# A fused attention and low-rank mixer kernel: eight seven-product pairs in each of batches 1 to 3, low-rank steps shared by two head pairs, part of one VectorE add moved to ScalarE, and a new written-out order

## The chip, the cores and the metric

The kernel runs on one core of one Trainium2 chip. The core has a matrix engine (TensorE, PE in the profile; its weight loads stand in a row of their own, PEld), VectorE (DVE), ScalarE (ACT), GpSimd (POOL) and a queue engine (SyncE, SP). Each runs its own instructions in the order in which they were issued and waits for others through semaphores. TensorE writes to PSUM, eight banks of 512 fp32 values on each of 128 partitions. The metric is the device time of one execution in microseconds (us). It was taken three times without the profiler, and once more with it.

## What is computed

Attention with a band of 96 positions and 8 global keys, for 4 batches, 8 heads, 768 positions and 64 values per head, and behind it a mixer: a low-rank product over positions (768 to 32 to 768) that is added to the attention's output, and a two-layer perceptron (512 to 2048 to 512) with a skip connection.

```python
# attention
scores = scale * np.matmul(q, k.transpose(0, 1, 3, 2)) + bias
scores = np.where(keep, scores, -1000000000.0)
a = np.exp(scores - max); a = a / (sum(a) + 1e-09)
attn = np.matmul(a, v)                    # 4 x 8 x 768 x 64
# mixer, x = attn as 4 x 768 x 512
xt = x.transpose(0, 2, 1)
h = xt @ U @ V                            # U 768 x 32, V 32 x 768
u = x + h.transpose(0, 2, 1)
out = u + np.maximum(u @ w_ch1, 0.0) @ w_ch2
```

## The kernel before

**Units of work.** Work is cut into tasks, each for one engine: a Python function that issues one to 22 instructions. A planner (`Planner.run`) goes through the task names in the order of the list `ORDER`, gives each the earliest start that its engine, its inputs and its buffers allow by costs written beside it (duration, `lat`, `lead`), and picks a buffer or PSUM bank for it. The tasks are then issued by planned start. So on each engine the tasks run in the order of `ORDER`; the costs set only the choice of banks and buffers and the order between engines in the program's text. The chip's own waits decide when each really starts.

**Attention.** Two heads form a pair; there are four pairs in a batch, numbered 0 to 15 through the four batches. For pair p: `lk`, `lq`, `lv` load keys, queries and values (GpSimd queue, with a cast to fp16); `TK`, `TQ` transpose on TensorE for pairs 0 to 7, and `EK`, `EQ` take the result out of PSUM; for pairs 8 to 15 `EK` and `EQ` are DMA transposes on SP's queue. `KO`, `VC`, `VG` make shifted copies of keys and values. `SB` and `S` are the scores, `EX` the exponential (ScalarE), `MK` a mask (VectorE), `PV` the product with the values, `RC` and `NM` the normalization into `x_sb`, `XC` a cast to fp16.

**Low-rank part.** `UP` multiplies a pair's cast output by U (six matmuls of 32 columns); `XE` copies the 32 columns four times side by side (ScalarE or VectorE), `XU` turns them on TensorE, `TE` copies them into `tmp`, and `HM` multiplies with V in row tiles of 32 partitions. From pair 4 on, `XT` turns the cast output itself with a DMA transpose (SP's queue) into `uT`, and `E0`, `E1` (line 1053 for a batch's last pair, line 1065 for the others) add the low-rank term from PSUM onto it with VectorE. `HM` is done for two pairs at once from pair 4 on.

**Perceptron.** The first layer multiplies `uT` by `w1` in 16 blocks of 128 hidden units, over two halves of 384 positions. Batch 0 does it plainly (`M1`, then `RL`, `RM` on ScalarE). In batches 1 to 3, blocks are taken in pairs (z and z+8) as 2 x 2 block products with seven products instead of eight (`ZP1` to `ZP7`, two matmuls of 384 columns each, line 1197), which need sums of weights (`ZS`) and of `uT` (`ZT`) from VectorE, three copies out of PSUM by ScalarE (`ZU`, `ZW`, `ZX`, line 410), three VectorE results (`ZA`, `ZB`, `ZD`, line 1214) and one ScalarE result (`ZR`, line 1242). Batch 1 has six such pairs and four plain blocks (hidden blocks 0, 1, 8 and 9), batches 2 and 3 have eight pairs. The second layer is done the same way in all batches: `Sa` to `Sd` are sums of hidden values (VectorE, line 1259), `RS` puts the low-rank term into PSUM first (line 1302), `P1` to `P7` are the products, each of eight matmuls of 256 columns (line 1319), for three blocks of positions t, and `DA` to `DH` (lines 1331, 1350, 1363) add them onto `x_sb`. `O` stores 128 positions (SP's queue).

**Names.** `P43.2b` is product 4 of batch 3, block 2, second half; `ZP21.4` is product 2 of batch 1, pair 4. Four tilings of TensorE occur: full (most), 64 rows (`S`), 32 rows (`HM`, `RS`) and one for the transposes of pairs 1 to 3.

## Time and profile before

| | |
|---|---|
| three executions without profiler | 214.19, 214.19 and 213.17 us (median 214.19) |
| the profiled execution | 213.56 us |
| its span, first to last instruction | 211.8 us |
| TensorE busy | 204.8 us (97%), 2231 matmuls |
| VectorE busy | 185.6 us (88%), 382 instructions |
| ScalarE busy | 135.2 us (64%), 255 instructions |
| GpSimd busy | 74.2 us (35%) |
| granted TensorE clock | 0.998 |

The page lists busy time by engine, the span in 40 slices, the DMA queues, the chain of work that ended last, and groups of instructions by source line with their mean duration. The duration of a matmul in the profile holds its way through the array, so neighbours overlap: what a run of matmuls costs is the length of the run in the chain, divided by their number. Further views give the busy time of each engine in chosen windows, the chain in order of time, waits with their releasers, and the time from a DMA's issue to its landing.

### The profile page before, as it was taken

What the parts mean: (1) busy time and instruction counts of PE and PEld (TensorE: products, weight loads), DVE (VectorE), ACT (ScalarE), POOL (GpSimd) and SP (SyncE); (2) the same over time, 40 slices, a digit from 0 to 9 for tenths busy, and PEclk for the clock granted to TensorE, in tenths of its full rate; (3) what the DMA queues carried; (4) which work ended last, traced back from release to release, by engine and by line L of the source; (5) the groups of instructions that cost most, each with busy time, mean ns of one, the idle gap of its engine ahead of it and who ended that gap; (6) DMA issues with size and microseconds to landing.
All of it is one profiled execution on the core that took longest, in us unless ns stands there. A gap on an engine that the chain in (4) does not pass through costs nothing.

```text
span 211.8 us, 5602 instructions
## 1 busy us (share of the span) xinstructions
PE 204.8 (97%) x2231; PEld 146.0 (69%) x2231; DVE 185.6 (88%) x382; ACT 135.2 (64%) x255; POOL 74.2 (35%) x98
## 2 busy tenths in 40 slices
...
GB/s 182 161 173 167 181 166 168 187 200 206 158 161 129 154 172 195 247 108 161 79 127 165 113 170 151 165 60 52 64 30 47 40 0 184 19 0 0 64 186 151
DMA packets 102330, 27.22 MB, mean 129 GB/s; under 512 B 90272, under 2 KB 99424, under 8 KB 102304
## 3 DMA queue, kind: packets, MB, share of 16 engines
...
q1 hardware_dynamic: 30112, 13.28, 30.1%
q8 instruction: 17, 0.28, 0.6%
...
HBM read 27.75 MB, written 6.29 MB: 161 GB/s over the span
## 4 chain that ended last, share of the span: by engine, by line
PE 83%; DMA 9%; POOL 3%; DVE 2%; issue 1%; POOLq 0%; DVEq 0%
PE ps L1319 33%; PE ps L1197 24%; PE ps L1103 9%; PE ps L774 4%; PE ps L1127 4%; DMA uT<-x 3%; DMA vt<-in_v_dram 3%; DMA stgk<-in_k_dram 2%; PE ps L908 2%; PE ps L907 2%; PE ps L1302 2%; PE ps L645 1%; PE ps L891 1%; PE ps L1020 1%; POOL stgq L501 1%
## 5 line engine op out<-in xcount | busy, mean ns | idle before, releaser
L839 ACT ACTIVATE ep<-ps 128x1024 f16<-128x1024 f32 (+1 forms) x48 | 44.3, 956 | 16.6 <-PE ps L774 16.4
L1319 PEld LDWEIGHTS <-htr 128*128 128x128 f16 x392 | 36.6, 98 | 6.4 <-issue 1.6
L1331 DVE TENSOR_TENSOR x_sb<-x_sb,ps 128x256 f32<-128x256 f32 (+1 forms) x60 | 26.5, 463 | 3.9 <-PE ps L1319 3.5
L410 ACT ACTIVATE zu<-ps 128x384 f32<-128x384 f32 x50 | 23.4, 497 | 9.8 <-PE ps L1197 6.4
L1319 PEld LDWEIGHTS <-sA 128*128 128x128 f16 x288 | 26.7, 97 | 3.7 <-issue 0.6
L1214 DVE CUSTOM_DVE_ANT_0 htr<-ps,zu 128x384 f16<-128x384 f32 x50 | 26.3, 550 | 1.8 <-PE ps L1197 1.8
L505 POOL DMA_DIRECT2D stgq<-in_q_dram x24 | 20.0, 852 | 21.6 <-DMA qT<-stgq 18.3
L1319 PE MATMUL ps<-w,sA 128*128 128x256 f16 x192 | 24.6, 273 | 0.0
L1197 PEld LDWEIGHTS <-w 128*128 128x128 f16 x176 | 16.8, 98 | 10.8 <-issue 0.2
L505 POOL DMA_DIRECT2D stgk<-in_k_dram x24 | 20.2, 857 | 11.5 <-DMA kT<-stgk 8.5
L1319 PE MATMUL ps<-w,htr 128*128 128x256 f16 x192 | 24.0, 273 | 0.0
L1319 PE MATMUL ps<-tB,htr 128*128 128x256 f16 (+1 forms) x200 | 23.3, 268 | 0.0
L1103 PE MATMUL ps<-uT,w 128*128 128x384 f16 x112 | 20.5, 326 | 0.0
L1197 PE MATMUL ps<-uT,w 128*128 128x384 f16 x88 | 19.5, 326 | 0.0
L1197 PE MATMUL ps<-zt,w 128*128 128x384 f16 x88 | 19.2, 326 | 0.0
L509 POOL DMA_DIRECT2D vt<-in_v_dram x16 | 16.8, 1058 | 4.0 <-PE ps L774 2.0
L852 DVE TENSOR_TENSOR ep<-ep,mask 128x1024 f16<-128x1024 f16 x24 | 16.3, 682 | 0.9 <-ACT ep L839 0.9
L946 DVE TENSOR_TENSOR x_sb<-ps,rcp 128x768 f32<-128x768 f32 x16 | 15.2, 953 | 0.4
L1103 PEld LDWEIGHTS <-w 128*128 128x128 f16 x112 | 10.5, 98 | 6.7
L1197 PE MATMUL ps<-zt,zs 128*128 128x384 f16 x64 | 14.6, 326 | 0.0
L774 PE MATMUL ps<-qT,kT 64*128 64x128 f16 x192 | 14.3, 218 | 0.0
L1109 ACT ACTIVATE htr<-ps 128x384 f16<-128x384 f32 x28 | 13.0, 495 | 1.9 <-PE ps L1103 1.5
...
## 6 DMA issues: line engine op xcount, KB each, us to landing
out_dram<-x_sb SPq DMA_DIRECT2D x22, 256.0 KB, 2.4
...
stgk<-in_k_dram POOLq DMA_DIRECT2D x24, 96.0 KB, 5.7
stgq<-in_q_dram POOLq DMA_DIRECT2D x24, 96.0 KB, 5.7
w<-in_moe_w_ch_dram POOLq DMA_DIRECT2D x8, 256.0 KB, 6.3
w<-in_moe_w_ch_dram POOLq DMA_DIRECT2D x4, 512.0 KB, 11.5
...
```

Of the source, the lines that this page charges most:

```text
L410: nc.scalar.activation(dst, src, AF.Copy)
L505: nc.gpsimd.dma_start(o[:, i], src[b, h0 + i].rearrange("(n p) d -> p n d", p=P))
L509: nc.gpsimd.dma_start(vt[gv.slot][:, :, :, 0:D], v[b, h0:h0 + 2].rearrange("h (n p) d -> p h n d", p=P),)
L774: nc.tensor.matmul(t[:, hi, j * P:(j + 1) * P], lhs, qt[r, i * P:(i + 1) * P], start=not biased, stop=True, skip_group_check=biased,)
L839: nc.scalar.activation(ep[gep.slot][:, :, lo:512], ps[:, gsc.slot:gsc.slot + 2, lo:512], AF.Exp, scale=qk_scale)
L852: nc.vector.tensor_tensor(ev, ev, mv, ALU.mult)
L946: nc.vector.tensor_tensor(xo, pvo()[:, :, :, 0:D], rcp[p % 2].unsqueeze(3).broadcast_to((P, 2, NB, D)), ALU.mult)
L1103: nc.tensor.matmul(ps[:, g.slot, 0:HS], w1[:, dc, jt * P:(jt + 1) * P], ub[:, dc, i * HS:(i + 1) * HS], start=(dc == 0), stop=(dc == NDC - 1),
L1197: nc.tensor.matmul(bank(g), a()[:, i], bq[:, i], start=first and i == 0, stop=last and i == 1, skip_group_check=True,)
L1214: return lambda: nc.vector._custom_dve(TENSOR_ADD_SAT, out=o, in0=x(), in1=y(), s0=3.0e38, s1=0.0)
L1319: nc.tensor.matmul(o if part is None else o[:, part], a[:, j, c0 + cols.start:c0 + cols.stop], bq[:, j] if part is None else bq[:, j, part ...
L1331: nc.vector.tensor_tensor(o, o, x, ALU.add)
```

## The change

- **Seven-product pairs.** Batch 1 takes all eight pairs with seven products; its four plain blocks and their `RL`, `RM` go. The sums `ZS0` of the weights, made in batch 2 before, are made in batch 1.
- **Shared low-rank steps.** Two neighbouring pairs put their `UP` results side by side (64 columns) into one PSUM bank of their own; one `XE`, `XU` and `TE` serve both (sixteen of each become eight), and `HM` is done for two pairs everywhere (ten become eight). `tmp` and `td` shrink to half. `DF` says which pair of the two comes first.
- **`RS`** changes from four matmuls of 32 rows and 256 columns to eight of 64 rows and 128 columns, with zeros in the rows of V that do not belong (`vz` and a longer `vs2` on VectorE make them once).
- **Low-rank term.** For nine pairs (`EA`) ScalarE copies the term from PSUM into an fp16 buffer (`AH`), and VectorE adds it from there (`E0`).
- **Engines of single tasks.** On VectorE no longer: `EK1 EK5 EK7 EQ1 EQ3 EQ7 KO7` and `VC10 VG10 VC15 VG15` (to ScalarE), `VC9 VG9 KO9` (to SP's queue); newly on VectorE: `EK3 EK6 KO11 KO14 VC6 VG6 XC10 XC15` (from ScalarE), `VC12 VG12` (from SP). `VC14 VG14` go from ScalarE to SP, `KO15` from SP to ScalarE.
- **Planner.** Other constants, a cost for early matmuls, another rule for SP's DMAs, one more filling matmul in gaps at the start.
- **Order.** `ORDER` is new throughout. Below are the places that the text speaks of.

The diff, cut to these parts:

```diff
 ORDER = """
...
-UP5 P30.0 DF0.1 MK7.0 EQ8 DF0.0 XT4 UP4 P50.2 XE4 P60.1 EK10 DA0.2 Sc0.1 XU4 ZS2 P60.2 PV7 XE5 TE4 RC7 DB0.2 NM7 XC6
-UP6 XE6 P60.0 XU5 XU6 TE5 P50.0 P70.2 DB0.1 lk11 DC0.0 TE6 DD0.2 XC7 P70.1 DB0.0 HM5 UP7 XE7 P40.2 P70.0 XU7 VC11 KO10
-TE7 KO8 XT6 XT7 E04 DD0.1 lk12 P50.1 DG0.2 E05 DD0.0 HM7 DC0.2 P40.0 P40.1 E06 S8.1 E17 E07 DG0.1 DG0.0 O0.0 lq9 DC0.1
-EK9 lv8 lq10 EX8.2 EX8.1 M1a1.1 O0.2 ZT1 M1b1.1 S8.0 M1b1.5 ZS3 EX8.0 ZP11.5 ZP11.6 lv9 ZP11.7 RM1.5 lv10 ZP21.5 ZU1.5
...
-P63.2 DC3.1 O2.3 O2.4 DF3.0 P33.1 DB3.2 DB3.1 O2.5 DF3.1 DD3.0 O2.0 P73.2 P73.1 DD3.2 O3.2a O2.1 O3.0 P43.0 DD3.1 O3.1
-O2.2 P43.1 P43.2a DG3.0 O3.5a DG3.1 DG3.2a O3.3 O3.4 P33.2 O3.5b DH3.2 O3.2 P43.2b DG3.2b O3.5c
...
+SB3.0 S3.2 S3.0 VC2 VG2 EX2.0 RC0 NM0 PV2 VC3 VG3 XC0 EX3.2 RC2 NM2 XC2 EX3.0 SB3.1 S3.1 UP0 EX3.1 UP1 w1_1 lq5 PV3.0
+PV3.1 lq4 XE1 lk4 XU1 TE1 w1_2 TQ5 w1_3 HM1 lv6 w1_0 lv5 lk5 PV3.2 TQ4 lv4 w1_5 lk6 w1_6 w2_2 w1_4 EQ5 E00 w1_7 E01
+w2_0 lq6 RC3.1 RC3.0 NH3.0 NH3.1 RC3.2 NH3.2 UP2 UP3.0 UP3.1 UP3.2 EQ4 XE3 mask1 NM3 TK4 XU3 M1a0.2 TE3 vz HM3 EK4 E02
+M1c0.2 M1a0.3 E13 M1c0.3 M1d0.3 E03 M1b0.3 M1d0.2 mask3 KO4 M1b0.7 mask2 M1b0.2 RL0.3 RL0.2 S4.1 EX4.1 M1b0.5 RM0.5
+M1b0.4 EX4.2 M1a0.1 M1a0.6 M1b0.6 TK5 RM0.7 M1a0.7 RM0.4 RL0.6 MK4.1 vs2 MK4.2 VC6 VC4 VG6 VG4 ZS1 VC5 RL0.7 mask4 EK5
...
+PV6 VC7 DF0.0 EX7.1 XC5 TWb1 P50.0 P30.2 XC4 RC6 NM6 S7.0 RS0.1 EX7.0 XT5 EQ8 MK7.2 EK8 MK7.1 VG7 DA0.2 MK7.0 P20.1
+DF0.2 XT4 P10.1 DC0.2 PV7 UP5 XC6 UP4 RC7 P30.1 UP6 XE5 DA0.1 XU5 P60.1 NM7 XC7 DF0.1 Sc0.1 DB0.1 P60.2 TE5 HM5 AH4
+UP7 AH5 XT7 P60.0 P50.1 ZS3 XT6 lk11 XE7 DB0.2 XU7 TE7 P70.1 E04 HM7 DB0.0 KO8 AH6 lv9 P70.2 lq11 E05 lv12 lq10 lq9
+ZP11.5 E17 E07 S8.1 EX8.1 ZU1.5 DD0.1 P70.0 P40.1 ZP11.0 ZP11.4 VC8 DD0.2 E06 EX8.2 ZP21.4 ZT1 DC0.0 ZP21.5 ZA1.5 VC9
+EK11 ZP61.5 DG0.1 DD0.0 VC10 ZW1.5 P40.2 DC0.1 ZP21.0 ZU1.4 ZP71.5 ZU1.0 P40.0 ZA1.4 ZA1.0 ZX1.5 ZP61.4 ZW1.4 DG0.0
+ZP51.5 DG0.2 ZB1.5 O0.2 S8.0 EX8.0 ZP11.6 ZP71.4 ZP41.5 O0.1 ZP31.5 ZP21.2 TD1 EK10 ZS0 ZP11.2 VG10 EK9 O0.0 ZX1.4
...
+P73.1 P33.0 DD3.1 DF3.0 DG3.2a O3.1 P43.1 P33.2 O3.0 DH3.2 P73.0 O3.5a O3.5b DG3.1 DD3.0 P43.2b DG3.2b O3.2 O3.4 O3.5c
+P43.0 DG3.0 O3.3
...
-    "Z": ((1, (2, 3, 4, 5, 6, 7)), (2, (0, 1, 2, 3, 4, 5, 6, 7)), (3, (0, 1, 2, 3, 4, 5, 6, 7))),
-    "ZK": (2, 3, 0, 1),
+    "Z": ((1, (0, 1, 2, 3, 4, 5, 6, 7)), (2, (0, 1, 2, 3, 4, 5, 6, 7)), (3, (0, 1, 2, 3, 4, 5, 6, 7))),
+    "ZK": [2, 3, 0, 1],
...
-    "TE": "AAADADAAAADAAADA",
-    "XE": "ADDAAAAAAAAAAAAA",
-    "EK": "ADDADDADAADAAAAD",
-    "EQ": "DDADADADADADAAAA",
-    "KO": "ADDDDDDDADAAASAS",
+    "TE": "AAAAAAAAAADAAADA",
+    "XE": "AADAAAADAAAAAAAA",
+    "EK": "AADDDADAAADAAAAD",
+    "EQ": "DAAAADAAADADAAAA",
+    "KO": "ADDDDDDAASADASDA",
...
-    "VO": "DDDDDDAADDDASAAD",
-    "XC": "DDDDAAAAAAAAQAAA",
+    "VO": "DDDDDDDADSAADASA",
+    "XC": "DDDDAAAAAADAQAAD",
...
-    "H2": [4, 6, 8, 10, 12, 14],
-    "R2": {0: (), 1: (), 2: (), 3: ()},
     "SG": [2, 2, 2, 4],
+    "EA": [4, 5, 6, 8, 9, 10, 12, 13, 14],
+    "DF": [0, 0, 1, 0, 0, 0, 0, 0],
...
-    OVER = {ACT: 0.105, DVE: 0.08}
+    COLD = 4.9
+    OVER = {ACT: 0.12, DVE: 0.09}
...
+            if t.eng == PE and s < self.COLD:
+                t.dur = min(2 * t.dur, t.dur + self.COLD - s)
...
-                    behind = max(0.0, dma_free[POOL] - s - 0.8)
-                    begin = max(s + t.lead, dma_free[SP])
-                    dma_free[POOL] = max(dma_free[POOL], begin) + need
-                    dma_free[SP] = begin + need
-                    t.end = begin + need + min(0.7 * behind, 6.0) + (1.1 if late else 0.3)
+                    behind = max(0.0, dma_free[POOL] - s)
+                    dma_free[POOL] = max(dma_free[POOL], s + t.lead - 0.8) + need
+                    t.end = s + t.lead + min(0.8 * behind, 6.5) + (0.4 if late else 0.1)
                     clock[SP] += min(0.08 * behind, 0.6)
...
-    tmp = sb("tmp", [P, DM], FP16, 2)
+    tmp = sb("tmp", [P, 2 * P], FP16, 2)
...
-    td = sb("td", [P, hd], FP16)
+    td = sb("td", [P, P], FP16)
...
+    c_vz = add(DVE, 0.55, lambda: nc.vector.memset(vs[:, 1:3], 0.0), name="vz")
...
-            o = vs[VR[g]:VR[g] + 2 * R, g]
-            if g < 2:
-                for i in range(2):
-                    nc.gpsimd.dma_start(o[i * R:(i + 1) * R], moe_V[:, g * HS:(g + 1) * HS])
-            else:
-                nc.vector.tensor_tensor(o, vf[:, 0:HS], vf[:, HS:S], ALU.subtract)
+            for i in range(2):
+                if g < 2:
+                    r = slice(64 * g + i * R, 64 * g + (i + 1) * R)
+                    nc.gpsimd.dma_start(vs[r, 0], moe_V[:, g * HS:(g + 1) * HS])
+                else:
+                    r, r2 = slice(i * R, (i + 1) * R), slice(64 + i * R, 64 + (i + 1) * R)
+                    nc.vector.tensor_tensor(vs[r, 1 + i], vf[r, 0:HS], vf[r, HS:S], ALU.subtract)
+                    nc.vector.tensor_copy(vs[r2, 1 + i], vs[r2, 0])
         return go
...
-        gu = Group("ps", 1, among=MLP1) if turned else gx
+        k = p % 2
+        if k == 0:
+            shared[p // 2] = Group("ps", 1, among=MLP1), Group("xu")
+        gu, gxu = shared[p // 2]
+        leads = CFG["DF"][p // 2] == k
 
         def low(a, b):
-            if turned:
-                return ps[:, gu.slot, a:b]
-            return ps[:, gx.slot + a // P, 384 + a % P:384 + a % P + b - a]
+            return ps[:, gu.slot, a:b]
 
...
-                        low(0, R), xx[:, c], u16[:, c],
-                        start=turned and c == 0, stop=(c == NB - 1), skip_group_check=True,
+                        low(k * R, (k + 1) * R), xx[:, c], u16[:, c],
+                        start=leads and c == 0, stop=(c == NB - 1), skip_group_check=True,
...
-        def hmix(k=0, gx=gx):
+        def hmix(gx=gx):
             for half in (0, 1):
                 r = slice(64 * half + R * k, 64 * half + R * (k + 1))
                 nc.tensor.matmul(
-                    ps[:, gx.slot + half, 0:HS], tmp[b % 2][r, hp * P:(hp + 1) * P], vs[r, half],
+                    ps[:, gx.slot + half, 0:HS], tmp[b % 2][r, hp // 2 * P:(hp // 2 + 1) * P], vs[r, 0],
                     start=turned, stop=True, skip_group_check=True,
...
+            f_, l_ = (ups[p], ups[p - 1]) if leads else (ups[p - 1], ups[p])
+            l_[0].deps.append(f_[-1])
+
+            def xuevac():
+                copy(
+                    ENG[CFG["XE"][p]], xus[gxu.slot].rearrange("p (g x) r -> p g (x r)", g=2),
+                    low(0, 2 * R).unsqueeze(1).broadcast_to((P, 2, 2 * R)),
+                )
+
+            def xuturn():
+                nc.tensor.matmul(
+                    low(P, 2 * P), xus[gxu.slot].rearrange("p g r -> p (g r)"), ident16, start=True, stop=True, skip_group_check=True,
+                )
+
+            def tevac():
+                copy(ENG[CFG["TE"][p]], tmp[b % 2][:, hp // 2 * P:(hp // 2 + 1) * P], low(P, 2 * P))
+
+            XE = add(ENG[CFG["XE"][p]], 0.28, xuevac, [f_[-1], l_[-1]], acq=[gxu], name=f"XE{p}")
+            XU = add(PE, 0.06, xuturn, [XE], lat=0.22, rel=[gxu], name=f"XU{p}")
+            TE = add(ENG[CFG["TE"][p]], 0.29 if CFG["TE"][p] == "D" else 0.3, tevac, [XU] + xw, rel=[gu], name=f"TE{p}")
+            other, og = waiting[p - 1]
+
+            def hboth():
+                other()
+                hmix()
+
+            HM = add(
+                PE, 0.19, hboth, [TE, c_vs[0], c_vs[1]], lat=0.22, acq=[og, gx] if turned else [], mode=2, name=f"HM{p}",
+            )
+            tmp_done[p - 1] = tmp_done[p] = TE
 
         def evacs(HM, gx=gx, turned=turned, XT=XT):
             w = mm1_done[b - 2] if b >= 2 else []
...
+            elif p in CFG["EA"]:
+                gh = Group("zu")
+
+                def low_copy():
+                    nc.scalar.activation(
+                        zu[gh.slot].bitcast(FP16).rearrange("p (h c) -> p h c", h=2), ps[:, gx.slot:gx.slot + 2, 0:HS], AF.Copy
+                    )
+
+                def low_add():
+                    o = uT[b % 2][:, hp]
+                    nc.vector.tensor_tensor(o, o, zu[gh.slot].bitcast(FP16), ALU.add)
+
+                AH = add(ACT, 0.81, low_copy, [HM], acq=[gh], rel=[gx], name=f"AH{p}")
+                ut_done[p] = (add(DVE, 0.555, low_add, [AH] + w + XT, rel=[gh], fast=2, name=f"E0{p}"),)
...
-            def rest(k, t, gXY=gXY):
-                gX, gY = gXY[t]
-                cols = slice(t * P, (t + 1) * P)
+            def rest(gX=gX, gY=gY, cols=cols):
                 for i in range(2):
-                    for n, g, m in ((1, gX, td if i else tb[:, 0:hd]), (2, gY, tb[:, i * hd:(i + 1) * hd])):
-                        r = slice(VR[n] + k * R, VR[n] + (k + 1) * R)
-                        yield half(g, i), vs[r, n, cols], m[r], i == 0
-
-            duo = CFG["R2"].get(b, ())
-
-            def rests(ts):
-                def go():
-                    for steps in zip(*(rest((k + ts[0]) % 2, t) for k, t in enumerate(ts))):
-                        for o, l, r, first_ in steps:
-                            nc.tensor.matmul(o, l, r, start=first_, stop=False, skip_group_check=True)
-                return go
-
-            if t not in duo[1:]:
-                ts = duo if t in duo else (t,)
-                RS = add(
-                    PE, 0.23 * (1.1 if t in duo else 1), rests(ts), [TD] + mm1_done[b][-1:] + c_vs, lat=0.3,
-                    acq=[g for u in ts for g in gXY[u]], mode=2, name=f"RS{b}.{t}",
-                )
-                rs_done[b].append(RS)
-                rs_of.update({(b, u): RS for u in ts})
-            RS = rs_of[b, t]
+                    for k in range(2):
+                        for r, g, m in ((slice(64, P), gX, td if i else tb[:, 0:P]), (slice(0, 64), gY, tb[:, i * P:(i + 1) * P])):
+                            nc.tensor.matmul(
+                                half(g, i)[:, k * P:(k + 1) * P], vs[r, 1 + k, cols], m[r], start=i == 0 and k == 0, stop=False, skip_group_check=True,
+                            )
+
+            RS = add(PE, 0.23, rest, [TD] + c_vs, lat=0.22, acq=[gX, gY], mode=1, name=f"RS{b}.{t}")
+            rs_done[b].append(RS)
 
...
-                    idle(int(gap / 0.43), 512, bank)
+                    idle(int(gap / 0.43 + 0.6), 512, bank)
...
```

198 lines of the change are left out of this document (84 added, 114 removed).

## Prediction

> **What bounds the kernel now.** I read the page's busy times first, then its summary of the chain, then the busy time of each engine in windows.
>
> ```profile
> PE 204.8 (97%) x2231; PEld 146.0 (69%) x2231; DVE 185.6 (88%) x382; ACT 135.2 (64%) x255; POOL 74.2 (35%) x98
> ...
> PE 83%; DMA 9%; POOL 3%; DVE 2%; issue 1%; POOLq 0%; DVEq 0%
> ```
> ```profile
> 15.00:20.00 5.00, 4.56 (x91) 2.81 (x88) 4.43 (x11) 4.51 (x7) 5.00 (x7) 1.00 2.26 171
> ...
> 70.00:80.00 10.00, 8.94 (x97) 6.89 (x96) 8.54 (x18) 5.41 (x10) 7.68 (x9) 1.00 2.15 161
> 80.00:90.00 10.00, 10.00 (x67) 5.89 (x66) 9.86 (x25) 8.00 (x18) 1.64 (x2) 1.00 1.68 225
> 90.00:100.00 10.00, 10.00 (x130) 6.20 (x129) 9.65 (x21) 9.80 (x18) 4.29 (x5) 1.00 1.53 133
> 100.00:110.00 10.00, 10.00 (x129) 7.86 (x127) 9.93 (x16) 7.64 (x15) 8.12 (x10) 1.00 1.50 109
> ```
>
> The columns are the window, its length, then busy time and instructions of PE, PEld, DVE, ACT and POOL, then the granted clock. TensorE is the bound: it stands in 83% of the chain, and from 80 us on it has no hole. It has holes in the start, where GpSimd issues loads without pause, and in one place between 70 and 80 us. But VectorE is nearly as full as TensorE in batch 1 (9.65 to 9.93 of 10). So a saving on TensorE counts in full only while VectorE keeps up. The chain in order of time (start, length, what) gives the hole and the prices:
>
> ```profile
> 27.27 0.65 PE ps L1127 x4
> ...
> 54.81 0.32 PE ps L1302 x4
> 55.13 0.98 PE ps L1319 x8
> ...
> 66.67 0.06 PE ps L1000
> ...
> 71.32 6.52 DMA uT<-x
> 77.93 1.03 DVE uT L1053 x2
> 79.00 1.46 PE ps L1127 x8
> ...
> 123.09 0.55 PE ps L774 x16
> ...
> 166.28 0.87 PE ps L1319 x8
> 167.16 0.27 PE ps L1020 x4
> 167.43 0.98 PE ps L1319 x8
> ...
> 172.01 17.23 PE ps L1197 x106
> 189.23 0.71 PE ps L1302 x12
> ...
> 208.45 0.29 DVE x_sb L1350
> ```
>
> **TensorE's own work.** A matmul of 384 columns costs 17.23 / 106 = 0.163 us. Eight blocks of a product cost 0.87 when the array keeps its tiling and 0.98 behind an `HM` or `RS`: leaving another tiling costs 0.11. Entering costs about the same: three `RS` together take 0.71, alone each 0.32, so 0.25 goes with two interruptions. I take 0.10 for each change of tiling.
> - Two more seven-product pairs: 32 matmuls of the first layer become 28, 4 x 0.163 = -0.65.
> - `XU`: eight fewer, six of them behind the start, 6 x 0.06 = -0.35.
> - Changes of tiling, counted by walking the two lists with the tilings of `S`, `RS`, `HM` and the early transposes: 101 before and 81 after in all; from the first task of layer one 70 and 60. `RS` now has the tiling of `S` and often stands next to it. 10 x 0.10 = -1.0.
> - `RS` itself: two matmuls run at once in different rows in both forms. Sixteen `S` matmuls of 128 columns take 0.55 with one change of tiling, 0.056 a couple, so eight take 0.22; four of 256 columns take 0.32 - 0.10 = 0.22. No difference.
>
> Against the last point stands a rule of the Trainium skill ("TensorEngine Tiling (Array Packing)", Instruction Overhead): each matmul carries some 60 cycles of overhead, so one should not cut a dimension that is small already. Read as an addition of 25 ns each (60 cycles at the 2.4 GHz that the Trainium skill gives in "Trainium Kernel Development and Optimization", NeuronCore Architecture), two more couples in each of twelve blocks would add an estimated 0.6 us, and the forecast would be 0.6 later. The trace speaks against that reading: a couple of 128 columns takes 0.056 us, half of what one of 256 columns takes.
>
> Together -2.0 us behind the start.
>
> **The hole at 78 us.** The last cast of batch 0 (`XC7`) ends at 71.3, its DMA transpose lands 6.52 us later, VectorE adds (`E17`, `E07`, 1.03), and TensorE starts layer one at 79.00 after 1.1 us of idleness.
>
> ```profile
> PE ps L1127 <- DVE uT L1053: 1.1, 1, 1.1
> ```
> ```profile
> DMA to landing us min/median/max: 2.7/4.3/7.1
> ```
> ```profile
> 67.80 5.33 SPq L987 DMA_TRANSPOSE uT<-x  x2
> ```
>
> In the new order I add up what TensorE has between the end of `XC7` and the first task that needs the transposes. By the list `XC7` ends some 3.4 us after `PV7` starts. `P40.1` stands 10.0 us of TensorE work after `PV7`, so the cover is 6.6 us. `P40.1` needs `DD0.1`, which VectorE has queued behind `E17` and `E07`: landing + 0.55 + 0.55 + 0.41, less overlaps, about landing + 1.3. At a landing of 6.5 us the stall is 1.3, as before; at the median of 4.3 there is none. `XT6` is now issued behind `XT7` on SP and blocks `E06` and with it `ZP21.4`, which has 1.5 us more cover. Fewer loads are queued just ahead of `XT7` than before, so I take a landing of 5.7 and a stall of 0.5: -0.7 (ends -1.24 and +0.3).
>
> At the other two batch boundaries there is no hole now. `XT11` stands behind `EK12` on SP and `DD1.1` behind `E111`, `E011`; `XT15` stands behind `XT13`, and `DD2.0` behind `E115`. With landings as above this gives nothing to 1.5 us in sum; +0.4.
>
> **VectorE and ScalarE.** The nine low-rank adds, the extra products and the moves of tasks are priced by these rows (mean ns after the comma):
>
> ```profile
> L1065 DVE TENSOR_TENSOR uT<-uT,ps 128x768 f16<-128x768 f16 x9 | 8.4, 949 | 0.4 <-issue 0.2 <-PE ps L1020 0.2
> L1156 DVE TENSOR_TENSOR zt<-uT,zt 128x768 f16<-128x768 f16 x3 | 1.7, 557 | 0.1
> L1214 DVE CUSTOM_DVE_ANT_0 htr<-ps,zu 128x384 f16<-128x384 f32 x50 | 26.3, 550 | 1.8 <-PE ps L1197 1.8
> L412 DVE COPY vo<-vt 32x660 f16<-32x660 f16 x10 | 4.6, 463 | 0.1
> L412 DVE COPY vo<-vt 128x660 f16<-128x660 f16 x10 | 4.0, 407 | 0.8 <-DMA vt<-in_v_dram 0.8
> L412 DVE COPY qT<-ps 128x768 f16<-128x768 f16 x4 | 3.0, 746 | 3.9 <-PE ps L645 3.9
> L412 DVE CAST x<-x_sb 128x768 f16<-128x768 f32 x3 | 1.6, 542 | 0.0
> L1179 DVE TENSOR_TENSOR w<-w 128x512 f16<-128x512 f16 x4 | 1.7, 425 | 0.1
> ```
> ```profile
> L410 ACT ACTIVATE uT<-ps 128x768 f16<-128x768 f32 x3 | 2.4, 811 | 0.1
> L410 ACT ACTIVATE xus<-ps 128x128 f16<-128x128 f32 x14 | 3.8, 276 | 7.9 <-PE ps L891 7.8
> ```
>
> An add that reads PSUM takes 0.949, one of the same shape from SBUF 0.557: nine pairs give VectorE -3.5. Six more `ZA`, `ZB`, `ZD` cost 6 x 0.55 = +3.3. Of `EK` and `EQ` four more leave than come, -3.0; five `XE` and `TE` go, -1.4; two `XC` come, +1.1; `vz` and the longer `vs2` are about three more copies like those of 0.4, +1.3; one `VC`, `VG` couple goes, -0.9. In all about -3.1, mostly in the start and in batch 0. ScalarE gets 9 x 0.81 = +7.3 and four `EK`, `EQ`, +3.2, and loses eleven `XE`, `TE`, -3.0, and some copies; at 64% it is not near a bound. The nine copies stand behind `HM`, and the transposes that the adds wait for as well land later than the copies end, so they add nothing to the path while that holds; without that cover it is 0.81 + 0.56 - 0.95 = 0.4 us per boundary.
>
> The Trainium skill ("VectorE: DVE Perf Modes", Rules for kernel authors) says to accept the slow rate on a matmul's output, or to copy it out of PSUM first if many operations use it; here one does. By that rule the copies would not pay: with batch 1's three adds as slow as before, the stall below would be 1.2 us longer and the forecast 213.6. The two rows of the trace differ from it as far as VectorE alone goes (0.557 against 0.949).
>
> In batch 1, however, VectorE gains work: the six products, `ZS0` (4 x 0.425 = 1.7, from batch 2) and `VC12`, `VG12` (0.87), less 3 x 0.39 and `VC9` to `VG10` (1.74) and `KO9`. Neighbours on VectorE overlap: two adds of 0.413 take 0.74, so I take 0.09 off each.
>
> ```profile
> 78.87 0.74 DVE L1331 TENSOR_TENSOR x_sb<-x_sb,ps 128x256 f32<-128x256 f32 x2
> ```
> ```profile
> L1331 DVE TENSOR_TENSOR x_sb<-x_sb,ps 128x256 f32<-128x256 f32 x49 | 19.2, 413 | 3.1 <-PE ps L1319 3.0
> ```
>
> Summed that way along the lists, from `ZP11.5` to the first `RS` of batch 1 the new order holds 23.7 us of TensorE work and 24.6 of VectorE work; the old one 21.5 and 18.5. The next stretch, to batch 2's first `ZP`, has slack again (26.0 and 22.6). I take a stall of 0.5, between nothing and 2.0.
>
> **The start.** The new list has 0.44 us less TensorE work and ten changes of tiling less ahead of layer one, and 3 us less VectorE work. But holes lie there already, and loads decide:
>
> ```profile
> 14.20 1.88 POOL L505 DMA_DIRECT2D stgk<-in_k_dram  x2
> ```
> ```profile
> stgk<-in_k_dram POOLq DMA_DIRECT2D x24, 96.0 KB, 5.7
> ```
>
> `lk4` is issued from 14.20. In the new order `u16`, `w1_1`, `lq5`, `lq4` are ahead of it (`u16` comes from an earlier place), 5 us more of GpSimd's issue time, so it lands near 26. `TK4` stands behind `UP3.2` and just before `XU3` and `M1a0.2`; layer one began at 27.3 before. So the start gains little: -0.4, from -1.4 (all of the work saved) to +1.0 (a late load ahead of `TK4` or `TQ4`, in TensorE's queue, with all of `UP3` behind it).
>
> **The end.** Before, the last product was half a block (`P43.2b`), with an add of 0.29 and a store of 64 KB behind it. Now `P43.0` is last, with an add of 0.41 and a store of 256 KB.
>
> ```profile
> out_dram<-x_sb SPq DMA_DIRECT2D x22, 256.0 KB, 2.4
> ...
> out_dram<-x_sb SPq DMA_DIRECT2D x2, 64.0 KB, 1.7
> ```
>
> That is +0.12 + 0.7. `P43.0` also waits for `DD3.0` with only `P43.2b` as cover: +0.1. Sum +0.9, between +0.1 and +1.1.
>
> **Sum.** -2.0 - 0.7 + 0.4 + 0.5 - 0.4 + 0.9 = -1.3. The profiled execution took 213.56 (0.6 below the median of the three without profiler, inside their spread); the four average 213.8. That gives 212.3 to 212.5; I say 212.4.
>
> **Rivals.**
> - *More is gained.* The loads let layer one begin a microsecond earlier, and the transposes land within their cover: 212.4 - 1.0 - 0.9 - 0.3 = 210.2. For it: VectorE's lighter start. Against it: GpSimd busy for 5.00 of 5 us from 15 to 20.
> - *VectorE becomes the bound in batch 1.* The 24.6 us against 23.7 are not caught up, since each `ZA` and `ZD` also frees a PSUM bank that TensorE waits for: +1.5 over my term, 213.9. For it: 9.9 of 10 now. Against: there was no hole at this load.
> - *The changes bring nothing.* Batch 0 is held by its loads up to the second layer, so what it saves is waited for there, and the stalls take the rest: about 213.6.
> - *Slower: late transposes.* At the two boundaries from batch 0 and from batch 1 the stall is the landing less 5.3 and, with `EK12` in front, less about 4.1. At 7.1, the longest landing, this is 1.8 + 3.0 instead of my 0.9: 216.3. It decides where the sum passes 3.8, from a landing of about 6.6 on at both. For it: 6.52 in the hole. Against: it was in the crowd of loads, and the median is 4.3.
>
> **Chances.** Forecast 0.50, more gained 0.12, VectorE 0.12, nothing 0.08, late transposes 0.18. Half a per cent, 1.1 us, is about what a measurement of this kernel can tell from no change. The first two are faster by more: 0.62; the next two within: 0.20; the last slower: 0.18. The forecast's own range is 211.0 to 213.1. The range that takes in the other cases, with the last one's far half left out, is 210.0 to 215.4.
>
> **What would show it.** Layer one of batch 0 should begin at 26 to 28 us; the windows of 80 to 190 us should show TensorE at 10 of 10; the hole near 78 should be under 0.8; `L1197` should count 28 matmuls more and line-1103 matmuls fewer; the store at the end should come 3.9 us behind the last product instead of 3.1. The prediction is wrong if TensorE idles over 1 us at a batch boundary on a DMA `uT<-x`, if it waits for VectorE in batch 1, or if the start takes 29 us.

## The result, and the profile after

The changed kernel is not faster but a little slower: 215.26 us (median of 20 executions, 213.97 to 216.57) against 214.42 (20, 213.11 to 218.87) for the kernel before, a ratio of 1.0049 with a 95% interval of 1.0025 to 1.0073. (The ratios, here and below, leave out executions in a slower state of the chip, into which every kernel falls now and then; the medians keep them.) Forecast were 212.4 us and a faster kernel. The profiled execution took 214.78 us, with a span of 212.9 (before: 213.56 and 211.8).

The page's busy times and the summary of the chain, after the change:

```profile
PE 204.8 (96%) x2275; PEld 148.0 (69%) x2275; DVE 183.3 (86%) x383; ACT 142.1 (67%) x257; POOL 74.2 (35%) x98
...
PE 76%; DVE 14%; DMA 3%; issue 2%; ACT 2%; POOL 1%; SPq 1%; DVEq 0%; POOLq 0%; ACTq 0%
```

TensorE's share of the chain fell from 83% to 76%, VectorE's rose from 2% to 14%. The windows (columns as in the prediction):

```profile
15.00:20.00 5.00, 4.87 (x83) 2.75 (x81) 4.75 (x14) 4.78 (x7) 4.81 (x6) 1.00 2.10 186
70.00:80.00 10.00, 10.00 (x104) 7.44 (x102) 9.07 (x22) 6.95 (x12) 8.60 (x10) 1.00 1.80 140
80.00:90.00 10.00, 9.57 (x67) 5.83 (x66) 9.32 (x23) 7.15 (x16) 0.00 (x0) 1.00 1.44 212
90.00:100.00 10.00, 10.00 (x88) 6.18 (x88) 9.88 (x23) 8.00 (x20) 2.58 (x3) 1.00 0.75 138
```

The hole at 78 us is gone; a smaller one has opened between 80 and 90. The chain in order of time shows how the execution began, where VectorE came in, and how it ended:

```profile
4.95 0.80 PE ps L649 x6
5.75 0.64 PE ps L1409 x6
6.39 0.64 PE ps L649 x6
7.03 1.92 PE ps L759 x6
8.95 0.47 PE ps L630 x12
9.45 0.81 ACT kT L412
10.26 0.71 ACT qT L412
...
71.80 5.70 DMA uT<-x
77.59 0.56 DVE uT L1075
...
80.06 0.68 DVE x_sb L1366
80.75 0.48 DVE htr L1233
81.27 0.81 PE ps L1216 x4
...
208.28 1.05 PE ps L1322 x8
209.35 0.42 DVE x_sb L1334
```

The 5.70 us are the landing of `XT6`. Behind it stand, on VectorE, its add `E06` (77.59), the sums `ZT1`, `DC0.0` (80.06) and `ZA1.5` (80.75), and then TensorE's `ZP21.0` (81.27). So VectorE's part of the chain begins at a late transpose.

Six transposes at the start take 0.64 from start to start, 0.107 each. In the kernel before, the second six (`TQ0`) took 0.33, from 6.31 to 6.64: TensorE there was at full speed from 6.2 us on, here only from 8.6. The page's granted clock says 1.00 in all these windows; the slow time is seen in the matmuls' spacing alone.

Where the time lies, from the starts of the tasks in each trace (us):

| | layer one begins | from there to the end of the last matmul | from there to the end |
|---|---|---|---|
| before | 27.11 | 181.30 | 3.37 |
| after | 28.78 | 180.54 | 3.60 |

### The profile page after: what moved, and what is told of

Its sections match the earlier page's. It is cut to its first block, busy times and chain, and to the rows that moved or that the text cites. A ratio compares the mean times of both kernels' runs of the same rounds, so it can differ in the third digit from the quotient of the medians.

```text
span 212.9 us, 5689 instructions
## 1 busy us (share of the span) xinstructions
PE 204.8 (96%) x2275; PEld 148.0 (69%) x2275; DVE 183.3 (86%) x383; ACT 142.1 (67%) x257; POOL 74.2 (35%) x98
## 4 chain that ended last, share of the span: by engine, by line
PE 76%; DVE 14%; DMA 3%; issue 2%; ACT 2%; POOL 1%; SPq 1%; DVEq 0%; POOLq 0%; ACTq 0%
PE ps L1322 26%; PE ps L1216 25%; PE ps L1122 7%; PE ps L778 5%; DVE x_sb L952 3%; DMA uT<-x 3%; DVE x_sb L1334 2%; PE ps L1146 2%; PE ps L914 2%; PE ps L649 2%; PE ps L913 2%; PE ps L759 1%; PE ps L1311 1%; DVE x_sb L1366 1%; DVE ep L856 1%
## 5 line engine op out<-in xcount | busy, mean ns | idle before, releaser
L1233 DVE CUSTOM_DVE_ANT_0 htr<-ps,zu 128x384 f16<-128x384 f32 x56 | 29.2, 551 | 2.6 <-PE ps L1216 2.3
L412 ACT ACTIVATE zu<-ps 128x384 f32<-128x384 f32 x56 | 25.7, 491 | 8.7 <-PE ps L1216 4.8
L1216 PEld LDWEIGHTS <-w 128*128 128x128 f16 x192 | 18.5, 98 | 12.4 <-issue 1.0
L1322 PE MATMUL ps<-tB,htr 128*128 128x256 f16 (+1 forms) x200 | 24.3, 268 | 0.2
L1322 PE MATMUL ps<-w,sA 128*128 128x256 f16 x192 | 23.9, 273 | 0.0
L1216 PE MATMUL ps<-zt,w 128*128 128x384 f16 x96 | 20.8, 326 | 0.1
L1216 PE MATMUL ps<-uT,w 128*128 128x384 f16 x96 | 20.0, 326 | 0.3 <-DVE htr L1233 0.3
L1122 PE MATMUL ps<-uT,w 128*128 128x384 f16 x96 | 17.4, 326 | 0.0
L1216 PE MATMUL ps<-zt,zs 128*128 128x384 f16 x72 | 16.8, 326 | 0.0
L1216 PEld LDWEIGHTS <-zs 128*128 128x128 f16 x108 | 10.5, 98 | 7.2 <-issue 0.4
L778 PE MATMUL ps<-qT,kO 64*128 64x128 f16 x160 | 12.7, 218 | 1.5 <-ACT qT L412 1.3
```

Source lines behind the costliest of these rows:

```text
L412: nc.scalar.activation(dst, src, AF.Copy)
L778: nc.tensor.matmul(t[:, hi, j * P:(j + 1) * P], lhs, qt[r, i * P:(i + 1) * P], start=not biased, stop=True, skip_group_check=biased,)
L1122: nc.tensor.matmul(ps[:, g.slot, 0:HS], w1[:, dc, jt * P:(jt + 1) * P], ub[:, dc, i * HS:(i + 1) * HS], start=(dc == 0), stop=(dc == NDC - 1),
L1216: nc.tensor.matmul(bank(g), a()[:, i], bq[:, i], start=first and i == 0, stop=last and i == 1, skip_group_check=True,)
L1233: return lambda: nc.vector._custom_dve(TENSOR_ADD_SAT, out=o, in0=x(), in1=y(), s0=3.0e38, s1=0.0)
L1322: nc.tensor.matmul(o if part is None else o[:, part], a[:, j, c0 + cols.start:c0 + cols.stop], bq[:, j] if part is None else bq[:, j, part ...
```

## The experiments

All are edits of the changed kernel, if nothing else is said. Banks and buffers are written down as the changed kernel has them, so that another order does not make the planner pick others, except for the tasks of a start that is reordered. All were timed against the kernel before on the same chip. One profiled execution is one sample, and the start differs from execution to execution; so averages decide, and the profile says why. The first idea was that ScalarE's chain of exps sets the start.

**Copies of pair 1 back on VectorE.**

```
-    "EK": "AADDDADAAADAAAAD",   "EQ": "DAAAADAAADADAAAA",
+    "EK": "ADDDDADAAADAAAAD",   "EQ": "DDAAADAAADADAAAA",
```

> The changed kernel with EK1 and EQ1 (the copies of pair 1's keys and queries out of PSUM) on VectorE, as before the change; order and buffers as changed. Changed kernel: layer one begins at 28.78 us, the first exp (EX1.2) at 11.44, the last of the start (EX3.1) ends at 24.23. Theory A (ScalarE's chain of twelve exps begins 3.2 us late because pair 1, whose data lands last, goes first): nothing is gained, since the two copies stand one behind the other on VectorE too (0.95 each there, 0.81 on ScalarE); EX1.2 between 11.4 and 11.8, layer one between 28.5 and 29.2. Rival B (the two copies in series on ScalarE are the delay): EX1.2 a microsecond earlier or more, layer one at 27.5 to 27.8. Rival C (loads or the shared low-rank step hold the start): layer one within 0.2 of 28.78 wherever the exps begin.

Measured: ratio 1.0092 (1.0054 to 1.0130). The exps began earlier (10.73) and ended later (24.92 instead of 24.23); layer one began at 29.32. In this execution TensorE was at full speed from 4.96 us, then idle from 8.5 to 10.3, and about a microsecond behind that its clock fell:

```profile
9.00:10.00 1.00, 0.00 (x0) 0.00 (x0) 1.00 (x3) 0.00 (x0) 1.00 (x3) 1.00 1.31 171
...
11.00:12.00 1.00, 1.00 (x14) 0.61 (x14) 0.00 (x0) 1.00 (x2) 1.00 (x2) 0.60 1.59 172
12.00:13.00 1.00, 1.00 (x8) 0.18 (x4) 0.00 (x0) 1.00 (x2) 1.00 (x2) 0.50 2.17 164
...
14.00:15.00 1.00, 1.00 (x26) 0.91 (x23) 0.28 (x1) 0.89 (x1) 0.52 (x2) 0.69 2.05 165
```

The granted clock (third column from the end) is 0.5 to 0.7 from 11 to 15. It was no chance of this one execution: in all eleven the mean granted clock lay between 0.988 and 0.992, in the unedited kernel at 0.998 or more. Rival B falls, and the loss itself comes from something that none of the three theories held.

**Pair 0 first again; the same with the copies; the start of before, as far as it fits.** In a first form none of the three fitted: there was no room for a buffer or a PSUM bank. The start of before as a whole does not fit beside the extra bank of the shared low-rank step.

```
-... EQ0.0 SB1.0 SB1.2 mask6 SB0.0 lq1 ... TK1 TQ1 EK1 EQ1 KO1 S1.2 S1.0 SB1.1 S1.1 S0.0 EX1.2 ...
+... EQ0.0 SB0.0 SB0.2 mask6 lq1 ... S0.0 EX0.0 SB0.1 TK1 S0.1 S0.2 TQ1 EK1 EX0.1 EQ1 EX0.2 ... S1.2 ...
```

> The changed kernel with pair 0 ahead of pair 1 again in scores, exps, PV and casts (the loads of the values swapped with them); EK1 and EQ1 stay on ScalarE; all behind it as changed. In the changed kernel the first exp begins at 11.44, the last of the start (EX3.1) ends at 24.23 and layer one begins at 28.78 us. Theory A (the chain of exps on ScalarE sets the start, and it begins 3.2 us late because pair 1, whose data lands last, goes first): EX0.0 begins near 8.6; twelve exps (11.6), EK1, EQ1, EQ2, EQ3 (3.3), less overlaps of 0.1 each, put the end of EX3.1 near 22.9, layer one at 27.3 to 27.9, and the time 0.9 to 1.5 us below the changed kernel's. Rival B (loads or the shared low-rank step hold the start): EX3.1 ends earlier, but layer one stays within 0.2 of 28.78 and the time within 0.3.

> Pair 0 first, and EK1 and EQ1 on VectorE. Theory A: the chain of exps begins near 8.4 and ScalarE has 1.6 us less in it; EX3.1 ends near 22, layer one begins at 26.5 to 27.2, 1.6 to 2.2 us before the changed kernel's 28.78, and the time falls by as much, to 0.3 to 0.6 per cent below the kernel before. Rival B: layer one at 28.6 or later. Rival D (the two copies on VectorE leave TensorE idle, and its clock falls behind that, as in the run with the copies alone): some granted clock under 1 between 10 and 16 us, and layer one later than in the run with pair 0 first alone.

> The start of the kernel before (order of the tasks ahead of layer one, loads included, and the engines of pairs 0 to 3), as far as the shared low-rank step allows it: its extra bank of PSUM puts UP0 behind EX3.2, and UP2, TQ4 behind HM1. All behind the start as changed. Theory A: layer one at 26.6 to 27.4, the time 1.4 to 2.1 us below the changed kernel's, so 0.2 to 0.5 per cent below the kernel before: what the change lost, it lost in its start. Rival B with the shared step as the cause: layer one stays at 28 or later although the exps and the loads are those of before. Rival B with the loads as the cause: layer one near 27 here, but at 28.6 or later in the two runs that keep the loads of keys and queries.

| | first exp | last exp of the start ends | layer one | ratio |
|---|---|---|---|---|
| pair 0 first | 7.96 | 26.27 | 30.63 | 1.0082 (1.0046 to 1.0118) |
| and copies on VectorE | 7.85 | 26.55 | 30.91 | 1.0110 (1.0078 to 1.0143) |
| start of before, as far as it fits | 7.73 | 22.99 | 27.98 | 1.0335 (1.0287 to 1.0384) |

Theory A falls: in the first two the exps began 3.5 us earlier and ended later. There `SB3.1` waited until 24.2 and 24.5 for the bank that `NM2` frees, a wait that this new order brought. In the third the exps ended 0.5 later than in the kernel before (22.50) and layer one began at 27.98. Its average says nothing of the start, for TensorE later waits 4.1 us for `KO5`, the shifted keys of pair 5: they stand on VectorE behind `VC6`, and the values of pair 6 that `VC6` copies land at 41.8 in that order of loads (28.6 in the changed kernel):

```profile
PE ps L814 <- DVE kO L450: 4.1, 1, 4.1
```

So an early first exp does not make an early layer one: in the first two runs a PSUM bank holds the chain up in between.

The first two runs show one thing more. Behind the start nothing is edited in them, and from `PV3.0` on TensorE has the same tasks in the same order. Yet from `ZP11.5` to the first `RS` of batch 1 they took 23.76 and 23.75 us, where the changed kernel took 24.63, and TensorE did not wait there. The windows of the changed kernel and, below them, of the run with pair 0 first:

```profile
80.00:84.00 4.00, 3.71 (x33) 2.47 (x32) 4.00 (x11) 2.31 (x6) 0.00 (x0) 1.00 1.82 205
84.00:88.00 4.00, 3.89 (x24) 2.24 (x23) 3.32 (x10) 3.35 (x7) 0.00 (x0) 1.00 1.36 184
```
```profile
80.00:84.00 4.00, 4.00 (x32) 2.91 (x31) 4.00 (x10) 2.77 (x6) 1.42 (x2) 1.00 2.53 156
84.00:88.00 4.00, 4.00 (x31) 2.28 (x29) 3.88 (x11) 3.25 (x7) 0.00 (x0) 1.00 1.34 200
```

Up to `E05`, 0.7 us ahead of `ZP11.5`, VectorE ran alike in pair 0 first and the changed kernel, within 0.02 us. What differs then is when transposes land: `XT7` 2.75 and 2.77 us after issue, against 4.53, and `XT6` 0.5 and 0.9 us earlier against `ZP11.5`. So `E06` began 0.5 and 0.6 us earlier, and VectorE's queue behind it ran that much ahead.

**`ZA1.5` ahead of `DC0.0`.** The first test of the stall at 80.7.

```
-... ZT1 DC0.0 ZP21.5 ZA1.5 VC9 ...
+... ZT1 ZP21.5 ZA1.5 DC0.0 VC9 ...
```

> The changed kernel with one task of VectorE moved past one other at the begin of batch 1's first layer: ZA1.5, which frees the bank that ZP21.0 waits for, goes ahead of the add DC0.0 (0.69). In the changed kernel ZA1.5 runs from 80.66 to 81.21, 0.88 after its product is done, and TensorE's ZP21.0 starts at 81.27 instead of 80.82. Theory (the stalls in batch 1 come from single places of VectorE's queue): the stall of 0.45 us goes, ZP21.0 starts near 80.8, the stretch from ZP11.5 to the first RS1 takes 24.2 instead of 24.63, and the time falls by 0.3 to 0.5 us. Rival (VectorE is the bound there, with 24.6 us of work against 23.7): the stall comes back at the next places, the stretch stays within 0.15 of 24.63, and the time within 0.2.

Measured: 1.0043 (1.0006 to 1.0080), against 1.0049 unedited. The wait moved to `P40.0` (0.54, for `DD0.0`), and `S8.1` waited 0.78 for a late `XT7`; the stretch took 25.43. Without those 0.78 it is 24.65, that of the unedited kernel: the stall moved on, as the rival has it. And in this execution, with nothing changed in the start, layer one began at 27.63 instead of 28.78. TensorE was at full speed from 4.95 us on. So 1.15 of the 1.67 us was not the order of the start, but the length of its slow time. What decides that?

**No hole ahead of the first transposes.** In the kernel before, the idle matmuls of the start are followed by `SB0.1` at 4.20; in the changed one TensorE is idle from 3.85 to 4.95.

```
-                    idle(int(gap / 0.43 + 0.6), 512, bank)
+                    idle(int(gap / 0.43 + 0.6) + 2 * (t.name == "TK0"), 512, bank)
```

> The changed kernel with nine instead of seven idle matmuls ahead of the first transposes, so that TensorE has no hole between 3.85 and 4.95 us (the kernel before has a bias product, SB0.1, there at 4.20). In the profiled execution of the changed kernel matmuls ran at half speed up to 8.6 us and layer one began at 28.78; in another execution with the same start at full speed from 4.96 and layer one began at 27.63; in the kernel before the speed doubled between 6.1 and 6.3. Theory W (the hole lets the slow time last a window longer in part of the executions): full speed by 7 us in the profile, layer one at 27.4 to 27.8, and on average 0.2 to 0.6 us off the time. Rival: the hole has no part in it; the speed changes anywhere between 5 and 8.6, and the average stays within 0.2.

Measured: 213.70 us, 1.0004 (0.9971 to 1.0038). The chain, filled start:

```profile
3.63 1.28 PE ps L1451 x3
...
4.95 0.80 PE ps L691 x6
5.75 0.64 PE ps L1451 x6
6.39 0.38 PE ps L691 x6
6.76 1.08 PE ps L801 x6
```

The six bias matmuls that took 1.92 take 1.08; layer one begins at 27.60.

**The same hole in the kernel before** (edit of the kernel before).

```
-... bias4 SB0.1 Ck0.1 TK0 Cq0.0 ...
+... bias4 Ck0.1 TK0 SB0.1 Cq0.0 ...      (and at most seven idle matmuls)
```

> The kernel before with one thing of the changed kernel: the bias product SB0.1 behind the first transposes instead of ahead of them, with the same seven idle matmuls, so that TensorE has a hole from 3.85 to 5 us. Theory W (such a hole lets the half-speed time last one window of about 3.4 us longer in some of the executions): on average 0.3 to 1.0 us slower than the kernel before; in the profile the speed is full from 5 us on, or half up to 8 or later, not from 6.2. Rival (the clock is no matter of this hole; what the filled start won came from elsewhere): within 0.2 us of the kernel before.

Measured: 0.9999 (0.9955 to 1.0043). In the profile the speed was full from 4.83 us on, which theory W allowed, but on average nothing was lost. The interval is as wide as the effect, so this left it open, and three more runs were made side by side.

**Unedited, wider hole, no hole, on one chip.** The second has four idle matmuls instead of seven (a hole from 2.6 us), the third nine.

```
+                    idle(int(gap / 0.43 + 0.6) - 3 * (t.name == "TK0"), 512, bank)     (wider)
+                    idle(int(gap / 0.43 + 0.6) + 2 * (t.name == "TK0"), 512, bank)     (none)
```

> The changed kernel once more, nothing edited, beside the next three on the same chip. If the hole in TensorE's start is the cause (theory W): the profile shows either full speed from 5 us and layer one near 27.6, or half speed to 8.6 us or later and layer one at 28.8 or later; the average near that of the first measurement, 0.5 per cent above the kernel before.

> The changed kernel with four instead of seven idle matmuls ahead of the first transposes: the hole in TensorE grows from 3.85 to 4.95 us to 2.6 to 4.95. Theory W: fewer executions are at full speed early; half speed to 8 us or later in the profile, layer one at 28.7 to 30, the average 0.2 to 0.8 us above the unedited changed kernel. Rival (the hole has no part): within 0.3 us of the unedited one, layer one anywhere between 27.6 and 28.8.

> The changed kernel with nine idle matmuls (no hole), as measured before on another chip, now beside the unedited one. Theory W: the double speed comes between 6 and 6.5 us, layer one at 27.5 to 28.0, the average 0.6 to 1.2 us below the unedited one. Rival: within 0.3 us of it.

| | full speed from | layer one | median (executions) | ratio |
|---|---|---|---|---|
| hole 3.85 to 4.95 | 9.7 | 29.71 | 215.41 (12) | 1.0050 (1.0017 to 1.0084) |
| hole 2.6 to 4.95 | 9.7 | 29.95 | 215.91 (6) | 1.0104 (1.0073 to 1.0135) |
| no hole | 4.2 | 27.66 | 213.90 (12) | 0.9999 (0.9973 to 1.0026) |

The chain of the unedited kernel in its second profile:

```profile
6.39 0.64 PE ps L691 x6
7.03 2.13 PE ps L801 x6
```

The order of the three is the one that theory W gave. The unedited kernel's twelve times fall into two groups, four from 213.58 to 213.93 and eight from 215.24 to 216.80; all six with the wider hole are at 215.61 or more, and all twelve without one at 214.97 or less. Over all profiles: with a hole, full speed came by 4.96 us in five and between 8.6 and 10.0 in six; without one it came by 6.9 in all nine. Only the time of the third was not as expected (earlier than 6). The Trainium skill ("TensorE: Matmul & The Clock Gate", Part 1: The HAM clock gate) says that the clock is halved until one window of about 3.4 us, which runs freely and not from the kernel's start, has been busy. The traces agree: a hole costs no window or one, as the phase has it. The later profiles lie between 5.3 and 6.9 us without a hole and between 8.6 and 10.0 with one, 3.1 to 3.3 further on.

**`EK8` behind `XT7`.** The rest of the miss lies at the begin of batch 1.

```
-... EQ8 EK8 XT4 XT7 XT6 (SP)     ZP11.5 S8.1 P70.0 P40.1 (PE)
+... EQ8 XT4 XT7 EK8 XT6 (SP)     ZP11.5 P70.0 S8.1 P40.1 (PE)
```

> The changed kernel with EK8 (the DMA that frees the buffer lk11 waits for) issued behind XT7 instead of ahead of XT4, and P70.0 ahead of S8.1 on TensorE. In the changed kernel lk11 is issued at 70.31, 0.2 us ahead of XT7, and five loads follow it; XT7 lands 4.53 us and XT6 5.70 us after issue, where 2.75 was measured for an XT7 with no load around it. Theory L (the boundary from batch 0 to batch 1 is held by transposes that land behind these loads): XT7 lands near 2.8 us and XT6 under 4 us after issue, E06 starts near 76 instead of 77.59, the stretch from ZP11.5 to the first RS1 takes 23.8 to 24.2 us instead of 24.63, and the time falls by 0.4 to 0.8. Rival V (VectorE's work is the bound there): the landings shorten, but the stretch stays at 24.4 or more. Rival K (S8.1 now waits for the later EK8): S8.1 starts 0.3 to 0.6 us later against ZP11.5 and the gain is lost there.

Measured: 1.0038 (1.0003 to 1.0074). `XT7` landed after 2.72 us and `XT6` after 2.79, as theory L has it, but `S8.1`, now behind `P70.0`, began 1.29 us behind `ZP11.5` instead of 0.42, and the exps of its scores kept the bank that `ZP21.4` needs (a stall of 0.65); the stretch took 24.84. The gain was lost at that place as rival K has it, though `EK8` itself was not late.

**More work for VectorE.**

```
-                    op(home[:, 1], A11, A21, ALU.subtract)
+                    for _ in range(4 if zp == 0 else 1):
+                        op(home[:, 1], A11, A21, ALU.subtract)
```

> The changed kernel with VectorE's first subtraction of ZS0 (0.425 us, in batch 1's first layer at 84.6) done four times instead of once, to the same values: 1.2 us more work for VectorE there and nothing else. Rival V (VectorE is the bound from ZP11.5 to the first RS1): that stretch grows from 24.63 by 0.9 to 1.2 us, and the time with it. Theory L (the stretch is held by the late landings ahead of it and VectorE has some slack behind): it grows by 0.4 or less.

Measured: 1.0065 (1.0038 to 1.0091); the stretch took 25.48, 0.85 more for 1.2 us of added work, between the two theories and near V. The stretch alone would not show it, since two executions of one kernel can differ as much there (24.72 and 25.57 with the filled start, below). But TensorE waits for just what was lengthened and for what stands behind it:

```profile
PE ps L1259 <- DVE zs L1242: 0.4, 1, 0.4
PE ps L1259 <- DVE htr L1276: 0.4, 1, 0.4
```

**Six pairs in batch 1 again** (with the filled start).

```
-    "Z": ((1, (0, 1, 2, 3, 4, 5, 6, 7)), ...
+    "Z": ((1, (2, 3, 4, 5, 6, 7)), ...        (units 0 and 1 as eight M1 halves, ZS0 behind DB1.0)
```

> The changed kernel with the filled start and with six seven-product pairs in batch 1 as before the change: units 0 and 1 are four plain blocks (32 matmuls for 28, 0.65 us more of TensorE, eight evacuations on ScalarE), ZS0 moves behind the first layer of batch 1; VectorE loses 6 x 0.55 + 1.7 = 5.0 us there. As predicted (two more pairs are worth 0.65 less a stall of 0.5): the stretch from ZP11.5 to the first RS1 takes 24.72 + 0.65 - 0.5, so about 24.9, and the time stays within 0.3 us of the run with the filled start. Rival V (the pairs bring nothing, since VectorE's work makes all of the stall of 1.0): 24.35 to 24.5, and the time 0.2 to 0.4 lower. Rival T (TensorE's work alone counts, the stalls are of the queue): 25.2 to 25.4, and 0.5 to 0.7 higher.

Measured: 1.0102 (1.0045 to 1.0158), stretch 26.62, outside all three. With 5 us less VectorE work TensorE waits elsewhere, for ScalarE's evacuations, and later for the add behind which `ZS0` now stands:

```profile
PE ps L1362 <- DVE x_sb L1374: 2.0, 2, 1.8
...
PE ps L1256 <- ACT zu L452: 0.6, 1, 0.6
```

The order was not fitted to the six pairs, so what the two pairs are worth stays open. It does show that VectorE's sum of work was not the only bound: less work in a queue that does not fit is no gain.

**VectorE's queue mended** (with the filled start), then two more moves, then the first once more beside a last edit.

```
-ZT1 DC0.0 ZA1.5 DG0.1 DD0.0 DC0.1 ZA1.4 ZA1.0 ... ZB1.4 ZA1.6 ... KO11 ... VC12      (DVE)
+ZT1 ZA1.5 DD0.0 DC0.0 DG0.1 DC0.1 ZA1.4 ZA1.0 ... ZA1.6 ZB1.4 ... (KO11 behind Sd1.1, VC12 behind DB1.1)
+ZT1 ZA1.5 DD0.0 DC0.0 ZA1.4 ZA1.0 DG0.1 DC0.1 ...                  (second run)
-EQ8 EK8 XT4 XT7        (SP)
+EQ8 XT4 EK8 XT7        (last run, on the first)
```

> The changed kernel with the nine idle matmuls of the filled start, and with VectorE's queue mended at the two places in batch 1 where TensorE waits: ZA1.5 and DD0.0 ahead of DC0.0; ZA1.6 ahead of ZB1.4, and ZP21.7 ahead of ZP31.4 on TensorE; KO11 and VC12 (0.74 us together) behind the first layer. In the run with the filled start alone the stretch from ZP11.5 to the first RS1 took 24.72 us against 23.7 of TensorE work, with stalls of 0.59, 0.31 and 0.14. Theory (single places of the queue): the three stalls go, the stretch takes 23.7 to 24.1, and the time falls by 0.6 to 1.0 us below the run with the filled start, to about 0.4 per cent below the kernel before. Rival V (VectorE has more work than TensorE up to the first RS1): the stalls move to other tasks, as when ZA1.5 alone was moved; the stretch stays at 24.4 or more.

> The kernel with the filled start and VectorE's mended queue, and one more move: ZA1.4 and ZA1.0 ahead of the adds DG0.1 and DC0.1, since S8.0 waited for the bank that ZA1.0 frees (0.34 us at 82.0, and 0.16 behind). Theory (single places of the queue): the two stalls go, the stretch from ZP11.5 to the first RS1 takes 23.8 to 24.0 instead of 24.30, and the time is 0.2 to 0.5 us below 0.9961 of the kernel before, near 0.994. Rival V: the stalls move on to other tasks, the stretch stays at 24.2 or more, the time at 0.996.

> The kernel with the filled start and VectorE's mended queue once more, unedited, beside the run above on the same chip. If its first measurement (0.9961 of the kernel before) holds: 0.994 to 0.999. If it was the chip: 0.999 to 1.002, like the filled start alone and like the run with two more moves.

> The kernel with the filled start and VectorE's mended queue, and EK8 issued behind XT4 instead of ahead of it. EK8 then lands near 71.2 instead of 68.8 and frees lk11's buffer only after XT7 is issued at 69.5. Theory L (XT7 lands late since lk11 is issued just ahead of it): lk11 issued near 71.5, XT7 lands 2.7 to 3.3 us after issue instead of 4.3 to 5.8, no stall of S8.1 in any execution (0 to 1.2 us in the executions shown so far), the average 0.2 to 0.5 us below the same kernel without this edit. Rival: the landing stays over 4 us, or it shortens and the time stays within 0.15, since TensorE then waits for VectorE further on.

| | stretch from `ZP11.5` to `RS1` | from layer one to the last matmul's end | median | ratio |
|---|---|---|---|---|
| filled start alone | 24.72 | 180.44 | 213.70 | 1.0004 (0.9971 to 1.0038) |
| filled start alone, again | 25.57 | 181.30 | 213.90 | 0.9999 (0.9973 to 1.0026) |
| queue mended | 24.30 | 179.84 | 213.05 | 0.9961 (0.9935 to 0.9988) |
| two more moves | 24.81 | 180.33 | 214.17 | 1.0002 (0.9973 to 1.0032) |
| queue mended, again | 24.50 | 180.02 | 213.37 | 0.9977 (0.9952 to 1.0003) |
| and `EK8` behind `XT4` | 24.18 | 179.69 | 213.01 | 0.9953 (0.9924 to 0.9983) |

By the stretch in the first profiles 0.4 of about 1.0 us of stalls could be ordered away; the second profile of the filled start has 25.57 because `S8.1` waited 1.2 us for `XT7`. By the averages the mending is worth about 0.3%, two runs against two on different chips. The two further moves gave it back: TensorE then has one stall of 0.66, for an add on the line of `DC0.1`. The last edit does to the landings what theory L says. Median time to landing of the three transposes from 66 to 80 us, ahead of it and with it:

```profile
uT<-x SPq DMA_TRANSPOSE x3, 4.8
```
```profile
uT<-x SPq DMA_TRANSPOSE x3, 2.8
```

`S8.1` no longer waits (0.33 in the run beside it). But `lk11` is not all that makes transposes late. In the changed kernel `XT4` landed 4.47 us after issue although `lk11` was issued 2.0 behind it; with pair 0 first, at the same distance, 2.80. The DMA view of the changed kernel from 66 to 80 us (what was moved in 40 slices of 0.35 us; then packets, MB and share of the queue called instruction) shows something else: the transposes' packets all but cease from 70.6 to 72.0.

```profile
GB/s 211 40 67 219 208 68 86 212 217 47 153 210 229 8 0 8 5 84 147 159 158 165 194 160 163 180 222 177 154 151 152 155 150 159 149 157 155 151 144 154
...
q8 instruction: 1, 0.02, 0.4%
```

That one packet, of 16 KB, began at 70.35. In 17 of the 18 profiles of the changed kernel and its edits such a pause of 1.0 to 1.5 us follows such a packet while a transpose is in flight, and a late landing with it, where no load need be in flight at all: `EQ8` after 3.99 us with pair 0 first, `EK8` after 4.25 in the last run. In the eighteenth (`EK8` behind `XT7`) nothing was in flight, and nothing landed late. In the changed kernel the pause hits `XT4`, and `XT7` comes behind it. The four runs in which `XT7` landed early had the pause off `XT4` and also `lk11` away from `XT7`, so no run says what each is worth.

In the last kernel the stretch took 24.18, with the mended queue and early landings; with the unmended queue and early landings it took 23.76 and 23.75 (pair 0 first). No run has the filled start, the unmended queue and `EK8` behind `XT4`. So the mending helps where transposes land late, and that it is needed where they land early is not shown. The last kernel is faster than the kernel before by 0.47% (0.17 to 0.76), where the changed kernel is slower by 0.49%. Its windows:

```profile
70.00:80.00 10.00, 10.00 (x103) 7.56 (x100) 9.52 (x23) 7.53 (x13) 8.27 (x10) 1.00 1.54 124
80.00:90.00 10.00, 9.82 (x66) 5.94 (x65) 9.44 (x23) 7.35 (x17) 0.32 (x1) 1.00 1.47 224
```

**The end as before.**

```
-P43.1 P33.2 O3.0 DH3.2 P73.0 O3.5a O3.5b DG3.1 DD3.0 P43.2b DG3.2b O3.2 O3.4 O3.5c P43.0 DG3.0 O3.3
+P73.0 DG3.2a O3.1 P43.1 DD3.0 P33.2 ... O3.4 O3.2 P43.0 DG3.0 O3.3 P43.2b DG3.2b O3.5c
```

> The changed kernel with an end like that of the kernel before: P73.0 and DD3.0 earlier, P43.0 ahead of P43.2b, and half a block with a 64 KB store last. As predicted (end +0.9 by the change): 0.8 to 0.9 us less. By the profiles (span from the last matmul's end: 3.37 before, 3.58 after, and 0.23 in which P43.0 waits for DD3.0): 0.2 to 0.5 less. The start is not touched; layer one near 27.6 if TensorE is at full speed from 5 us, near 28.8 if from 8.6 us.

Measured: 1.0030 (0.9993 to 1.0067), no difference that the intervals show from 1.0049. In the profile it takes 23.26 us from the first `RS` of batch 3 to the end, against 23.14 unedited. But the edit did not bring the old end back: the kernel before takes 22.62 there, and 3.37 from the last matmul on, where the edit takes 3.95. So what the old end as a whole is worth was not tested.

The ScalarE copy of the low-rank term was not undone by itself, so what it is worth stays open. In this order `HM7` takes the banks of `HM5`, which `AH4` and `AH5` had emptied by 73.04; it began at 74.38, while the add `E05` ended at 74.88. Without the copies it would have to wait for the adds.

## Why the prediction was wrong

Its time lay in the range, its direction was wrong. Of the 2.4 us between the profiled 214.78 and the forecast 212.4, the start makes +2.1, the part from layer one to the last matmul +0.9, and the end -0.6. Two of its own signs of being wrong came: layer one began at 28.78 instead of 26 to 28, and TensorE waited for VectorE in batch 1. By its steps:

- **The start: this step failed.** -0.4 was forecast, with loads as what decides; it was +1.67 in the profile, or +0.5 where TensorE comes to full speed early. The loads landed in time (`lk4` at 25.2, worked out near 26; `TK4` at 28.1 behind `UP3.2`). What was missed is the hole that the new order leaves between the idle matmuls and `TK0`, because `SB0.1` no longer stands there. The prediction read "less TensorE work and ten changes of tiling less" as time, in a place where the speed of TensorE hangs on not being idle. Both were to be seen: in the trace before, `SB0.1` begins at 4.20 and transposes go from 0.107 to 0.055 apart at 6.2; in the list, nothing but idle matmuls stands ahead of `TK0`. Filling the hole wins 0.5% (1.0050 to 0.9999 side by side), about 1.1 us. The other +0.5 of the start is not explained by a run: no order of the exps or of the old start that was tried won it back.
- **The stalls: right for the hole, under-sized in batch 1.** The hole at 78 us went altogether (-1.1; -0.7 was forecast), and TensorE waits there for `S8.1` instead, 0 to 1.2 us by the execution. In batch 1 the stretch took 24.63 and 24.85 in the two profiles of the unedited kernel against 23.7 of work, so about 1.0 instead of 0.5. VectorE was in it, by single tasks (`ZA1.5` behind `DC0.0`, `ZB1.4` ahead of `ZA1.6`), but its sum was no bound: with 24.6 us of work by the list it held up nothing in the two runs with pair 0 first (23.76 and 23.75), where the transposes landed early. The term was put down to VectorE's load; what made it was when VectorE could begin.
- **TensorE's own work: over-sized.** From layer one to the last matmul the forecast was -2.0 - 0.7 + 0.4 + 0.5 + 0.1 = -1.7. It was -0.76, -1.61 in the last kernel, and -2.18 with pair 0 first, where hardly a wait is left. With the waits taken out by the matmuls' starts (1.2 us before, 1.8 after, 0.5 with pair 0 first) this part is 180.1, 178.8 and 178.6 us long: an estimate of 1.3 to 1.5 saved instead of 2.0. `RS` has 0.3 of the difference: the twelve hold TensorE for 3.59 us instead of 3.31, where no difference was forecast (0.6 by the reading that the prediction turned down).
- **The end: over-sized.** +0.9 was forecast. The profile has +0.2 from the last matmul to the end and 0.23 for `P43.0` behind `DD3.0`, and from the first `RS` of batch 3 to the end 23.14 against 22.62, so +0.5.
- **Late transposes, the slower rival**: right that they cost, wrong in where. TensorE did not idle at the boundary out of batch 0, since other work stood there; it paid in the stretch behind, through `E06` and VectorE's queue, about 0.9 us by 24.63 against 23.76. That rests on profiles: the two medians with and without `EK8` behind `XT4` are 0.36 apart, within their intervals. It is part of why the kernel is not faster. That it is slower is the hole alone: with the hole filled it stands at 1.0004 and 0.9999, late transposes and all.
